# Short convolution, router and experts in one kernel: the inversion's moving operand from one product over three sections, the experts' one-hots written contiguously, past counts added by VectorE, the third block's preparation handed to the first block's loop

## Chip, cores and metric

The kernel runs on one core of one Trainium2 chip. The metric is the device time of one execution in microseconds (us); the median of three runs stands for a kernel. PE is TensorE's matmul side and PEld its weight load, DVE is VectorE, ACT ScalarE, POOL GpSimd and SP the queue that issues most DMAs.

## The reference

```python
# x: (8, 3584, 192) f32, weight: (8, 7); 8 experts, w1: (8, 192, 1024), w2: (8, 1024, 192)
w = softmax(weight)                                   # per head, over 7 taps
y[b, s, h, :] = sum_k w[h, k] * x_padded[b, s + k, h, :]   # causal, 8 heads of 24 channels
t = y.reshape(28672, 192); out = t
do = t @ w_skip > 0                                   # only these tokens go on
e = argmax(t @ w_gate); g = softmax(t @ w_gate)[e]    # one expert of 8 for each
out[do] = t + g * (relu(t @ w1[e]) @ w2[e])           # relu network 192 -> 1024 -> 192
```

## The kernel before

**First phase.** The batches 0 to 7 are taken one after the other. A batch's 3584 tokens lie as 30 columns of 120 partitions. `phase1_step(b)` runs over eight pairs of heads and half-batches: the convolution is a matmul with a banded matrix (`toep`, fp32, L393), which ACT copies into `ys`, and the rows are stored as the preliminary output. Between these steps it advances generators: the router of batch b-1 and the inversion of an earlier batch. A generator gives up its turn at each `yield`; written tables (`RR`, `IR`, `PICK`, `BGS`, `PSEQ`) say how many turns each step gives. Every engine works its own instructions strictly in the order in which this program issued them.

**Router.** `router` turns `ys` by matmuls (`tp`), multiplies by the gate weights (`pl`), turns back (`pb`) and leaves logits `lg`, 120 x 30 x 9. `slots` finds each token's expert and its place in that expert's list. DVE makes `lm`, `df`, `kq`, `km` and then `oh`, an fp16 one-hot of the expert over 30 columns x 8 experts. PE multiplies `oh` by a matrix of ones and by a triangular matrix into the PSUM tile `pr`, and adds the counts of past batches (`hist`) by a third, one-row product. DVE then runs a scan along `pr` (`run`), adds the rest (`rs`), masks with `oh`, and reduces to the slot `sl`. From the slot come a row `rf`, a column `qf` and three small fp16 factors `vv`, `gh`, `gl`, which carry the token number and the gate value.

**Inversion.** `invert(b)` turns "token to slot" into "slot to token" by matmuls. For each chunk of 8 columns (`IC`; four chunks a batch, the last of 6) DVE compares into the stationary operand `oa` and into the moving operand `ob`; `ob` has three sections of 72 columns: the one-hot of `qf` times `vv`, times `gh` and times `gl`. One product per token column adds to the PSUM tile `inv` (L646). After batch 4 (`REL`) the lists of the first two experts are read out of it (`inva`, `sidxa`), so that their first eight blocks can begin early.

**Blocks.** A block is up to 256 tokens of one expert. `gather` fetches its rows, `prep` scales and splits them into fp16 high and low parts (DVE: `yam`, `ysc`, ACT and DVE: `yt`) and turns them by DMA into `m`; `up` is the first expert product (PE `ph`, ACT `hh`, DVE `hl`), `down` the second (PE `po`, DVE `o`, POOL scatter). The first blocks run between the last two batches' routing and inversion: `weave` issues a block's rows and, after each quarter of `up`, a `tail_slot`. During batch 7's convolution `step7(h)` issues `PSEQ[h]` pieces of the preparation of the first three blocks (`prep_piece`); a preparation of 256 tokens has seven pieces. The table sums to 21.

Of the kernel before, what the change touches and what calls it, by code (L numbers as in the profile page):

```python
# [8 lines left out]
F16 = mybir.dt.float16  # L9
# [93 lines left out]
def conv_router_moe(ctx: ExitStack, tc: tile.TileContext, x, weight, w_skip, w_gate, w1, w2, out):  # L103
# [431 lines left out]
    def slots(b, lg):  # L535
        def t3(name):
            return wk1.tile([R, NC, E], F32, tag=name, bufs=1, name=f"{name}{b}")

        def t2(name, dt=F32, bufs=1):
            return wk1.tile([R, NC], dt, tag=name, bufs=bufs, name=f"{name}{b}")  # L540

        def bc(t):
            return t.unsqueeze(2).broadcast_to([R, NC, E])

        lm = t2("lm")
        nc.vector.tensor_reduce(out=lm, in_=lg[:, 0:NC, 0:E], axis=AX.X, op=ALU.max)
        yield
        nc.vector.tensor_tensor(out=lg[:, NC - 1, E:E + 1], in0=lg[:, NC - 1, E:E + 1], in1=live, op=ALU.min)
        df = t3("df")
        nc.vector.tensor_tensor(out=df, in0=lg[:, 0:NC, 0:E], in1=bc(lm), op=ALU.subtract)  # L550
        ex = t3("ex")
        nc.scalar.activation(ex, df, AF.Exp)
        yield
        kq = t3("kq")
        nc.vector.scalar_tensor_tensor(out=kq, in0=df, scalar=0.0,
                                       in1=pri[0:R].unsqueeze(1).broadcast_to([R, NC, E]),
                                       op0=ALU.is_equal, op1=ALU.mult)
        yield
        km = t2("km")
        nc.vector.tensor_reduce(out=km, in_=kq, axis=AX.X, op=ALU.min)  # L560
        yield
        nc.vector.scalar_tensor_tensor(out=km, in0=lg[:, 0:NC, E], scalar=0.0, in1=km,
                                       op0=ALU.is_le, op1=ALU.add)
        yield
        oh = wk1.tile([R, E, NC], F16, tag="oh", name=f"oh{b}")
        nc.vector.tensor_tensor(out=oh.rearrange("p e c -> p c e"), in0=kq, in1=bc(km), op=ALU.is_equal)
        yield HOP
        if in_tail:
            yield HOP
        pr = ps_ms.tile([P, 2, E, NC], F32, tag="ms", name=f"pr{b}")  # L570
        nc.tensor.matmul(pr[:, 0], ones16[0:R, :], oh, start=True, stop=False)
        nc.tensor.matmul(pr[:, 0, :, 0], ones32, hist[0:1, b, :], start=False, stop=True)
        nc.tensor.matmul(pr[0:R, 1], um1[0:R, 0:R], oh, start=True, stop=True)
# [17 lines left out]
        nc.vector.tensor_copy(hist[:, b + 1, :], run[:, :, NC - 1])
        yield
        if b == REL:
            nc.vector.tensor_tensor(out=cnta, in0=hist[:, b + 1, 0:NA], in1=eoff[:, 0:NA], op=ALU.subtract)
            yield
            nc.vector.scalar_tensor_tensor(out=hist[:, b + 1, 0:NA], in0=eoff[:, 0:NA], scalar=float(KH * P),
                                           in1=hist[:, b + 1, 0:NA], op0=ALU.add, op1=ALU.max)
        nc.vector.tensor_tensor(out=rs, in0=rs, in1=oh, op=ALU.mult)
        yield HOP
        sl = t2("sl")  # L600
        nc.vector.tensor_reduce(out=sl, in_=rs.rearrange("p e c -> p c e"), axis=AX.X, op=ALU.add)
# [10 lines left out]
        nc.vector.tensor_tensor(out=eq3(cmp), in0=stab, in1=bstart[:, b].unsqueeze(2).broadcast_to([P, E, QC]),  # L612
                                op=ALU.is_ge)
        rf = t2("rf", F16, 2)
        nc.vector.tensor_copy(rf, ri)
        qf = t2("qf", F16, 2)
        nc.vector.tensor_copy(qf, qi)

        gs, gd = t2("gs"), t2("gd")
        nc.vector.tensor_scalar(out=gs, in0=gt, scalar1=UNITS, scalar2=None, op0=ALU.add)  # L620
        vu, vv = t2("vu"), t2("vv", F16, 2)
        nc.vector.tensor_scalar(out=vu, in0=ai, scalar1=PACK - 1.0, scalar2=1.0, op0=ALU.mult, op1=ALU.add)
        nc.vector.tensor_scalar(out=gs, in0=gs, scalar1=UNITS, scalar2=GBIAS, op0=ALU.subtract, op1=ALU.subtract)
        nc.vector.tensor_tensor(out=vv, in0=vu, in1=vtab[0:R], op=ALU.mult)
        nc.vector.scalar_tensor_tensor(out=gd, in0=gt, scalar=GBIAS, in1=gs, op0=ALU.subtract, op1=ALU.subtract)
        nc.vector.tensor_scalar(out=gd, in0=gd, scalar1=1.0 / PACK, scalar2=UNITS, op0=ALU.mult, op1=ALU.add)
        gh, gl = t2("gh", F16, 2), t2("gl", F16, 2)
        nc.vector.tensor_tensor(out=gh, in0=gs, in1=vu, op=ALU.mult)
        nc.vector.tensor_scalar(out=gd, in0=gd, scalar1=UNITS, scalar2=GREST, op0=ALU.subtract, op1=ALU.min)
        nc.vector.scalar_tensor_tensor(out=gl, in0=gd, scalar=-GREST, in1=vu, op0=ALU.max, op1=ALU.mult)  # L630
        rq[b] = (rf, qf, vv, gh, gl)
# [3 lines left out]
    def invert(b, rf, qf, vv, gh, gl):  # L635


        due = []
# [1 line left out]
        def products(at):  # L640
            if due and due[0][0] <= at:
                _, c0, i, oa, ob = due.pop(0)
                for v in range(min(IL, NC - c0 - IL * i)):
                    w = c0 + IL * i + v
                    at_q = IL * i + v
                    nc.tensor.matmul(inv, oa[:, i, :, v], ob[:, at_q // QL, :, at_q % QL],  # L646
                                     start=(b in (0, REL + 1) and w == 0), stop=(b in (REL, B - 1) and w == NC - 1))

        def each(out, in0, t, c0, op):
# [13 lines left out]
        at = 0  # L663
        for c0 in range(0, NC, IC):
            oa = wk1.tile([R, IC // IL, P, IL], F16, tag="oa", bufs=3, name=f"oa{b}_{c0}")
            ob = wk1.tile([R, IC // QL, 3 * NG, QL], F16, tag="ob", bufs=3, name=f"ob{b}_{c0}")
            each(oa, iota_r, rf, c0, ALU.is_equal)
            yield
            each(ob[:, :, 0:NG, :], iota_q, qf, c0, ALU.is_equal)
            products(at)  # L670
            at += 1
            yield HOP
            for n, part in enumerate((gh, gl)):
                each(ob[:, :, (n + 1) * NG:(n + 2) * NG, :], ob[:, :, 0:NG, :], part, c0, ALU.mult)
            each(ob[:, :, 0:NG, :], ob[:, :, 0:NG, :], vv, c0, ALU.mult)
            products(at)
            due.extend((at + TLAG, c0, i, oa, ob) for i in range(IC // IL))
            at += 1
# [514 lines left out]

    routes.append(whole_route(B - 1))
    in_tail.append(1)
    gathered, prepped = AHEAD - 1, PREP0
    ahead = []
    while preps or begun[0] < PREP0:
        prep_piece()
    bg.extend(save_weights(e, wts[e]) for e in range(NA))  # L1200
    weave(up(blocks[0], weights_of(0)), first=(blocks[0], *FIRSTP[0]))
    for n in range(NBLK):
        k = blocks[n]
        if 0 < n < 5:
# [105 lines left out]
```

## Time and profile before

| | |
|---|---|
| runs | 684.56, 684.56, 689.15 us; median 684.56 us |
| the profiled execution | 686.43 us, span of its instructions 684.7 us |
| mean granted TensorE clock | 0.993 |
| busy | PE 656.2 us (96%), DVE 544.3 (79%), ACT 352.1 (51%), POOL 271.0 (40%) |
| DMA | 133.31 MB, mean 195 GB/s |

The span is the time from the first to the last instruction. A timeline row gives start, length, engine, line, operation, destination and sources, and in brackets the idle time of that engine just before it and what ended that. A group row gives busy time, mean nanoseconds of one instruction and that idle time in total. [...]

### The profile page before, as it was taken

What the parts mean: (1) busy time and instruction counts of PE and PEld (TensorE: products, weight loads), DVE (VectorE), ACT (ScalarE), POOL (GpSimd) and SP (SyncE); (2) the same over time, 40 slices, a digit from 0 to 9 for tenths busy, and PEclk for the clock granted to TensorE, in tenths of its full rate; (3) what the DMA queues carried; (4) which work ended last, traced back from release to release, by engine and by line L of the source; (5) the groups of instructions that cost most, each with busy time, mean ns of one, the idle gap of its engine ahead of it and who ended that gap; (6) DMA issues with size and microseconds to landing.
All of it is one profiled execution on the core that took longest, in us unless ns stands there. A gap on an engine that the chain in (4) does not pass through costs nothing.

```text
span 684.7 us, 17904 instructions
## 1 busy us (share of the span) xinstructions
PE 656.2 (96%) x6586; PEld 563.9 (82%) x6586; DVE 544.3 (79%) x1617; ACT 352.1 (51%) x762; POOL 271.0 (40%) x301
## 2 busy tenths in 40 slices
PE   8999998999697999989999999999999999999995
PEld 7667676766587898979999899999999899999995
DVE  8159999988989989886997897888888876666652
ACT  4776585558742334554464464564554644444421
POOL 4111111124113454644554554644544555554322
PEclk9999999999999999999999999999999999999999
DMA  7999999962941657466359369578567456999970
GB/s 214 322 322 313 300 286 326 326 217 66 246 145 47 161 143 153 89 181 182 82 170 216 89 175 193 105 175 177 126 181 157 132 148 175 272 291 330 326 211 15
DMA packets 169127, 133.31 MB, mean 195 GB/s; under 512 B 74320, under 2 KB 155986, under 8 KB 169028
## 3 DMA queue, kind: packets, MB, share of 16 engines
q1 hardware_dynamic: 157988, 110.26, 60.1%
q0 software_dynamic: 11040, 21.80, 11.8%
q8 instruction: 54, 0.88, 0.5%
q14 instruction: 45, 0.37, 0.2%
HBM read 69.70 MB, written 48.04 MB: 172 GB/s over the span
## 4 chain that ended last, share of the span: by engine, by line
PE 55%; DVE 0%; POOL 0%; POOLq 0%; issue 0%
PE ph L888 28%; PE po L939 27%; POOL out_dram L927 0%; DVE hl L911 0%; POOLq L1251 0%; DVE yt L859 0%; DVE o L925 0%
## 5 line engine op out<-in xcount | busy, mean ns | idle before, releaser
L909 ACT ACTIVATE hh<-ph 128x512 f16<-128x512 f32 x230 | 136.2, 593 | 227.1 <-PE ph L888 226.1
L888 PE MATMUL ph<-m,wt 128*128 128x256 f16 (+2 forms) x2000 | 210.0, 270 | 4.4 <-DVE hl L911 2.8
L888 PEld LDWEIGHTS <-wt 128*128 128x128 f16 (+1 forms) x2000 | 167.5, 98 | 38.7 <-issue 17.9
L939 PE MATMUL po<-wt,hh 128*128 128x192 f16 x1536 | 194.2, 246 | 0.0
L911 DVE SCALAR_TENSOR_TENSOR hl<-ph,hh 128x512 f16<-128x512 f32 x230 | 157.5, 686 | 40.9 <-ACT hh L909 40.5
L939 PE MATMUL po<-wt,hl 128*128 128x192 f16 x768 | 188.9, 246 | 0.0
L939 PEld LDWEIGHTS <-hh 128*128 128x128 f16 x1840 | 166.5, 98 | 1.1
L927 POOL DMA_INDIRECT out_dram<-o,sidx x82 | 85.8, 1046 | 138.7 <-DVE o L925 119.4
L829 POOL DMA_INDIRECT y<-out_dram,sidx x82 | 85.3, 1041 | 26.8 <-issue 10.1
L939 PEld LDWEIGHTS <-hl 128*128 128x128 f16 x920 | 90.0, 98 | 0.0
L393 PE MATMUL pc<-xs,toep 128*120 128x384 f32 (+1 forms) x224 | 77.3, 467 | 0.0
L925 DVE SCALAR_TENSOR_TENSOR o<-po,yf,y 128x192 f32<-128x192 f32 x115 | 47.2, 417 | 37.0 <-PE po L939 30.8
L859 DVE SCALAR_TENSOR_TENSOR yt<-y,ysc,yt 128x64 f16<-128x64 f32 x230 | 62.2, 313 | 14.8 <-ACT yt L853 13.2
L395 ACT COPY ys<-pc 120x768 f32<-120x768 f32 (+1 forms) x56 | 42.6, 761 | 40.7 <-PE pc L393 31.8
L853 ACT ACTIVATE yt<-y,ysc 128x192 f16<-128x192 f32 x115 | 51.4, 447 | 19.4 <-DVE ysc L362 13.8
L393 PEld LDWEIGHTS pc<-xs,toep 128*120 128x120 f32 x224 | 36.5, 183 | 14.1 <-issue 0.4
L854 ACT ACTIVATE yt<-y,ysc 128x128 f16<-128x128 f32 x115 | 44.8, 389 | 0.0
L338 DVE SCALAR_TENSOR_TENSOR wt<-raw,ar,wt 128x512 f16<-128x512 f32 x56 | 42.2, 759 | 1.4 <-ACT wt L327 1.4
L327 ACT ACTIVATE wt<-raw,ar 128x512 f16<-128x512 f32 x56 | 38.9, 724 | 5.3 <-DVE ar L362 5.3
L888 PE MATMUL ph<-m,wd 128*128 128x256 f16 (+3 forms) x440 | 40.6, 258 | 0.0
L939 PE MATMUL po<-wd,hh 128*128 128x192 f16 x304 | 38.4, 246 | 0.0
L888 PEld LDWEIGHTS <-wd 128*128 128x128 f16 (+1 forms) x440 | 32.9, 97 | 6.6 <-issue 3.4
(213 smaller groups left out, 778.8 us busy)
## 6 DMA issues: line engine op xcount, KB each, us to landing
wd<-wscr SPq DMA_DIRECT2D x44, 449.0 KB
wscr<-wt SPq DMA_DIRECT2D x84, 128.0 KB
xs<-in_x_dram SPq DMA_DIRECT2D x7, 1440.0 KB
xs<-in_x_dram SPq DMA_DIRECT2D x7, 1248.0 KB
out_dram<-ys SPq DMA_DIRECT2D x6, 1344.0 KB
out_dram<-ys SPq DMA_DIRECT2D x6, 1092.0 KB
raw<-in_moe_w_dram SPq DMA_DIRECT2D x32, 192.0 KB
raw<-in_moe_w_dram SPq DMA_DIRECT2D x8, 512.0 KB
```

The source lines that it names most:

```text
L393: nc.tensor.matmul(pc[0:R, i, 0:n * G], toep[:, h + i, :], xs[b, half][:, :, (h + i) * G:(h + i + 1) * G], start=True, stop=True)
L395: nc.scalar.copy(ys[b, half][0:R, :, h * G:(h + 2) * G].rearrange("p g (h c) -> p h g c", c=G), pc[0:R, :, 0:n * G].rearrange("p i (g c) - ...
L829: rows_apart(nc.gpsimd.indirect_dma_start(out=k.y[:, u, :], out_offset=None, in_=out[0:k.rows, :], in_offset=bass.IndirectOffsetOnAxis(ap= ...
L853: nc.scalar.activation(yt[:, u, 0:D], k.y[:, u, :], AF.Copy, scale=sc[:, u:u + 1])
L854: nc.scalar.activation(yt[:, u, 3 * P:], k.y[:, u, D - P:D], AF.Copy, scale=sc[:, u:u + 1])
L859: nc.vector.scalar_tensor_tensor(out=yt[:, u, o:o + b_ - a], in0=k.y[:, u, a:b_], scalar=sc[:, u:u + 1], in1=yt[:, u, a:b_], op0=ALU.mult, ...
L888: nc.tensor.matmul(ph[:, f % fs, :], wt[q, o + f * P:o + (f + 1) * P], k.m[q, m, 0:w], start=start, stop=stop, skip_group_check=split)
L909: nc.scalar.activation(hh, ph, AF.Relu)
L911: nc.vector.scalar_tensor_tensor(out=k.hl[:, f0:f0 + fs, 0:w], in0=ph, scalar=0.0, in1=hh, op0=ALU.max, op1=ALU.subtract)
L925: nc.vector.scalar_tensor_tensor(out=o[:, u, :], in0=part, scalar=f2[:, u:u + 1], in1=k.y[:, u, :], op0=ALU.mult, op1=ALU.add)
L927: rows_apart(nc.gpsimd.indirect_dma_start(out=out[0:k.rows, :], out_offset=bass.IndirectOffsetOnAxis(ap=k.si[:, u:u + 1], axis=0), in_=o[: ...
L939: nc.tensor.matmul(part, lhs[:, f, u * P:(u + 1) * P], wt[:, w + f * D:w + (f + 1) * D], start=(n == 0), stop=(n == 3 * NF - 1))
```

## The change

1. `ob`: DVE now compares into a tile `eq` of its own, and one product over the three sections makes `ob`: `eq` is read three times by a broadcast, against a tile `parts` that holds the three factors side by side in pairs of columns. It takes the place of three products, one for each section.
2. `oh` is stored as 30 columns x 8 experts in the order in which DVE computes it, so its write is contiguous. The two matmuls write `pr` as before with experts outermost, now with a pitch of 30 elements between consecutive results. The masking of `rs` reads `oh` with a pitch of 8 elements.
3. The one-row product of `hist` goes; DVE adds the 8 counts to `pr` in front of the scan.
4. At the start of the last batch's routing, the loop that issued what was left of the three preparations goes; what is left is handed to the first block's `weave`.

```diff
-        oh = wk1.tile([R, E, NC], F16, tag="oh", name=f"oh{b}")
-        nc.vector.tensor_tensor(out=oh.rearrange("p e c -> p c e"), in0=kq, in1=bc(km), op=ALU.is_equal)
+        oh = wk1.tile([R, NC, E], F16, tag="oh", name=f"oh{b}")
+        nc.vector.tensor_tensor(out=oh, in0=kq, in1=bc(km), op=ALU.is_equal)
...
-        nc.tensor.matmul(pr[:, 0], ones16[0:R, :], oh, start=True, stop=False)
-        nc.tensor.matmul(pr[:, 0, :, 0], ones32, hist[0:1, b, :], start=False, stop=True)
-        nc.tensor.matmul(pr[0:R, 1], um1[0:R, 0:R], oh, start=True, stop=True)
+        nc.tensor.matmul(pr[:, 0].rearrange("p e c -> p c e"), ones16[0:R, :], oh, start=True, stop=True)
+        nc.tensor.matmul(pr[0:R, 1].rearrange("p e c -> p c e"), um1[0:R, 0:R], oh, start=True, stop=True)
...
+        nc.vector.tensor_tensor(out=pr[:, 0, :, 0], in0=pr[:, 0, :, 0], in1=hist[:, b, :], op=ALU.add)
...
-        nc.vector.tensor_tensor(out=rs, in0=rs, in1=oh, op=ALU.mult)
+        nc.vector.tensor_tensor(out=rs, in0=rs, in1=oh.rearrange("p c e -> p e c"), op=ALU.mult)
...
+        parts = wk1.tile([R, NC // QL, 3, QL], F16, tag="parts", name=f"parts{b}")
...
-        nc.vector.tensor_tensor(out=vv, in0=vu, in1=vtab[0:R], op=ALU.mult)
+        nc.vector.tensor_tensor(out=parts[:, :, 0], in0=by(vu), in1=by(vtab[0:R]), op=ALU.mult)
...
-            each(ob[:, :, 0:NG, :], iota_q, qf, c0, ALU.is_equal)
+            eq = wk1.tile([R, IC // QL, NG, QL], F16, tag="eq", bufs=2, name=f"eq{b}_{c0}")
+            each(eq, iota_q, qf, c0, ALU.is_equal)
...
-            for n, part in enumerate((gh, gl)):
-                each(ob[:, :, (n + 1) * NG:(n + 2) * NG, :], ob[:, :, 0:NG, :], part, c0, ALU.mult)
-            each(ob[:, :, 0:NG, :], ob[:, :, 0:NG, :], vv, c0, ALU.mult)
+            nc.vector.tensor_tensor(out=ob[:, 0:n], op=ALU.mult,
+                                    in0=eq[:, 0:n].unsqueeze(2).broadcast_to([R, n, 3, NG, QL]),
+                                    in1=parts[:, g0:g1].unsqueeze(3).broadcast_to([R, n, 3, NG, QL]))
...
-    gathered, prepped = AHEAD - 1, PREP0
-    ahead = []
-    while preps or begun[0] < PREP0:
-        prep_piece()
+    gathered, prepped = AHEAD - 1, begun[0]
+    ahead = list(preps)
...
-    weave(up(blocks[0], weights_of(0)), first=(blocks[0], *FIRSTP[0]))
+    weave(up(blocks[0], weights_of(0)), ahead, PU, first=(blocks[0], *FIRSTP[0]))
```

The order of instructions before, on DVE, at the first two chunks of batch 0's inversion (a number behind a tile's name only tells buffers apart; the last figures are partitions x elements):

```order
L658 TENSOR_TENSOR oa_0_691<-iota_r,rf_671 120x1024
L658 TENSOR_TENSOR ob_0_692<-iota_q,qf_673 120x4x144
L658 TENSOR_TENSOR ob_0_692<-ob_0_692,gh_685 120x4x144
L658 TENSOR_TENSOR ob_0_692<-ob_0_692,gl_686 120x4x144
L658 TENSOR_TENSOR ob_0_692<-ob_0_692,vv_679 120x4x144
L658 TENSOR_TENSOR oa_8_750<-iota_r,rf_671 120x1024
```

And in the changed kernel, on DVE, from the new addition of the past counts on (rows in between left out are the same small ones as before) and at the same chunks:

```order
L584 TENSOR_TENSOR pr_610<-pr_610,hist 128x8
L586 SCALAR_TENSOR_TENSOR run_637<-smask,pr_610 128x240
...
L662 TENSOR_TENSOR oa_0_689<-iota_r,rf_672 120x1024
L662 TENSOR_TENSOR eq_0_692<-iota_q,qf_674 120x576
L680 TENSOR_TENSOR ob_0_690<-eq_0_692,parts_671 120x1728
L662 TENSOR_TENSOR oa_8_747<-iota_r,rf_672 120x1024
L662 TENSOR_TENSOR eq_8_750<-iota_q,qf_674 120x576
L680 TENSOR_TENSOR ob_8_748<-eq_8_750,parts_671 120x1728
```

Three rows become one at each of 32 chunks, and one row of 8 elements is new in each of 8 batches; no other row of DVE changes its place.

On PE, before, between the turning products of batch 0 (`tp`, from `ys`) and the next convolution product (`pc`):

```order
L571 LDWEIGHTS ones_105
L571 MATMUL pr_610<-oh_590,ones_105 128x240
L572 MATMUL pr_610<-hist,ones_96 128x8
L573 LDWEIGHTS um_238
L573 MATMUL pr_610<-oh_590,um_238 120x240
L393 MATMUL pc_0_4_618<-xs_0_183,toep 120x384 x2
```

And in the changed kernel at the same place:

```order
L574 LDWEIGHTS ones_105
L574 MATMUL pr_610<-oh_590,ones_105 128x30x8
L575 LDWEIGHTS um_238
L575 MATMUL pr_610<-oh_590,um_238 120x30x8
L393 MATMUL pc_0_4_617<-xs_0_183,toep 120x384 x2
```

The one-row product is gone in each of the 8 batches, and the results go out as 30 groups of 8 with a pitch; nothing else moves on PE.

On ACT, at the end of batch 7's convolution, where the third block's preparation (`yt_2373` from `y_2032`) is followed by the last weight pieces and the first block's first `hh`, the kernel before has:

```order
L327 ACTIVATE wt_1108<-raw_1378,ar_1878 128x512
L853 ACTIVATE yt_2373<-y_2032,ysc_2347 128x192
L854 ACTIVATE yt_2373<-y_2032,ysc_2347 128x128
L853 ACTIVATE yt_2373<-y_2032,ysc_2347 128x192
L854 ACTIVATE yt_2373<-y_2032,ysc_2347 128x128
L327 ACTIVATE wt_1108<-raw_1378,ar_1878 128x512 x3
L909 ACTIVATE hh_2412<-ph_0_2414 128x512
L477 COPY ya_0_2431<-tp_0_0_2432 128x480
```

The changed kernel has these eight rows in the same order, with other buffer numbers and line numbers; so have its queues of POOL and SP, row for row.

More of the change, by code (lines that the diff above doesn't have):

```diff
@@ L543, in bc, with by @@
             return t.unsqueeze(2).broadcast_to([R, NC, E])
+        def by(t):
+            return t.rearrange("p (g v) -> p g v", v=QL)
         lm = t2("lm")
@@ L620, in slots, with invert @@
         nc.vector.tensor_scalar(out=gs, in0=gt, scalar1=UNITS, scalar2=None, op0=ALU.add)
-        vu, vv = t2("vu"), t2("vv", F16, 2)
+        vu = t2("vu")
         nc.vector.tensor_scalar(out=vu, in0=ai, scalar1=PACK - 1.0, scalar2=1.0, op0=ALU.mult, op1=ALU.add)
         nc.vector.tensor_scalar(out=gs, in0=gs, scalar1=UNITS, scalar2=GBIAS, op0=ALU.subtract, op1=ALU.subtract)
-        nc.vector.tensor_tensor(out=vv, in0=vu, in1=vtab[0:R], op=ALU.mult)
+        nc.vector.tensor_tensor(out=parts[:, :, 0], in0=by(vu), in1=by(vtab[0:R]), op=ALU.mult)
         nc.vector.scalar_tensor_tensor(out=gd, in0=gt, scalar=GBIAS, in1=gs, op0=ALU.subtract, op1=ALU.subtract)
         nc.vector.tensor_scalar(out=gd, in0=gd, scalar1=1.0 / PACK, scalar2=UNITS, op0=ALU.mult, op1=ALU.add)
-        gh, gl = t2("gh", F16, 2), t2("gl", F16, 2)
-        nc.vector.tensor_tensor(out=gh, in0=gs, in1=vu, op=ALU.mult)
+        nc.vector.tensor_tensor(out=parts[:, :, 1], in0=by(gs), in1=by(vu), op=ALU.mult)
         nc.vector.tensor_scalar(out=gd, in0=gd, scalar1=UNITS, scalar2=GREST, op0=ALU.subtract, op1=ALU.min)
-        nc.vector.scalar_tensor_tensor(out=gl, in0=gd, scalar=-GREST, in1=vu, op0=ALU.max, op1=ALU.mult)
-        rq[b] = (rf, qf, vv, gh, gl)
+        nc.vector.scalar_tensor_tensor(out=parts[:, :, 2], in0=by(gd), scalar=-GREST, in1=by(vu),
+                                       op0=ALU.max, op1=ALU.mult)
+        rq[b] = (rf, qf, parts)
         if b < B - 1:
             nc.vector.scalar_tensor_tensor(out=brow, in0=cmp, scalar=float(S), in1=brow, op0=ALU.mult, op1=ALU.add)
-    def invert(b, rf, qf, vv, gh, gl):
+    def invert(b, rf, qf, parts):
         due = []
@@ L645, in products @@
                     at_q = IL * i + v
-                    nc.tensor.matmul(inv, oa[:, i, :, v], ob[:, at_q // QL, :, at_q % QL],
+                    nc.tensor.matmul(inv.rearrange("p (s q) -> p s q", s=3), oa[:, i, :, v], ob[:, at_q // QL, :, :, at_q % QL],
                                      start=(b in (0, REL + 1) and w == 0), stop=(b in (REL, B - 1) and w == NC - 1))
@@ L665, in invert @@
             oa = wk1.tile([R, IC // IL, P, IL], F16, tag="oa", bufs=3, name=f"oa{b}_{c0}")
-            ob = wk1.tile([R, IC // QL, 3 * NG, QL], F16, tag="ob", bufs=3, name=f"ob{b}_{c0}")
+            ob = wk1.tile([R, IC // QL, 3, NG, QL], F16, tag="ob", bufs=3, name=f"ob{b}_{c0}")
             each(oa, iota_r, rf, c0, ALU.is_equal)
             yield
-            each(ob[:, :, 0:NG, :], iota_q, qf, c0, ALU.is_equal)
+            eq = wk1.tile([R, IC // QL, NG, QL], F16, tag="eq", bufs=2, name=f"eq{b}_{c0}")
+            each(eq, iota_q, qf, c0, ALU.is_equal)
             products(at)
@@ L672, in invert @@
             yield HOP
-            for n, part in enumerate((gh, gl)):
-                each(ob[:, :, (n + 1) * NG:(n + 2) * NG, :], ob[:, :, 0:NG, :], part, c0, ALU.mult)
-            each(ob[:, :, 0:NG, :], ob[:, :, 0:NG, :], vv, c0, ALU.mult)
+            g0, g1 = c0 // QL, min(c0 + IC, NC) // QL
+            n = g1 - g0
+            nc.vector.tensor_tensor(out=ob[:, 0:n], op=ALU.mult,
+                                    in0=eq[:, 0:n].unsqueeze(2).broadcast_to([R, n, 3, NG, QL]),
+                                    in1=parts[:, g0:g1].unsqueeze(3).broadcast_to([R, n, 3, NG, QL]))
             products(at)
```

## The prediction

> **What bounds the kernel now.** I began with the busy times by stage; the columns are the stretch, its length, PE, PEld, DVE, ACT and POOL busy with counts, clock, DMA share and GB/s.
>
> ```profile
> span 684.7 us, 17904 instructions
> 80.00:120.00 40.00, 38.05 (x283) 27.49 (x282) 37.32 (x115) 26.81 (x55) 5.03 (x8) 1.00 0.98 298
> 120.00:160.00 40.00, 37.55 (x280) 27.13 (x279) 35.40 (x108) 22.18 (x49) 8.86 (x15) 1.00 0.76 236
> 160.00:200.00 40.00, 33.71 (x309) 26.38 (x308) 35.63 (x122) 29.79 (x70) 8.89 (x10) 0.96 0.57 160
> 200.00:240.00 40.00, 34.77 (x375) 32.45 (x373) 38.91 (x122) 11.75 (x28) 13.73 (x14) 1.00 0.46 122
> 302.00:677.00 375.00, 374.65 (x4107) 339.72 (x4106) 288.74 (x785) 181.38 (x391) 184.99 (x182) 1.00 0.72 181
> ```
>
> From 302 to 677 us PE is busy for 374.65 of 375 us, and the chain that ended last is there nothing but PE's two expert products, to within a few us of the end:
>
> ```profile
> 302.35 5.64 PE ph L888 x35
> ...
> 673.22 3.97 PE po L939 x48
> ```
>
> The change does not touch that stretch, so it moves as a whole, by what is won before it. From 80 to 240 us PE idles 1.95 + 2.45 + 6.29 + 5.23 = 15.9 us, with DVE busy 147 of 160 us. The time can come only from these holes and from PE's own instructions. The groups and the timeline of PE name the holes:
>
> ```profile
> L571 PE MATMUL pr<-oh,ones 120*128 120x240 f16 x8 | 2.1, 264 | 6.8 <-DVE oh L566 6.8
> L646 PE MATMUL inv<-ob,oa 120*128 120x216 f16 x240 | 31.9, 262 | 4.4 <-DVE ob L658 4.4
> 109.37 0.26 PE L571 MATMUL pr<-oh,ones 120*128 120x240 f16 x1 [1.95 <-DVE oh L566]
> 141.78 0.55 PE L646 MATMUL inv<-ob,oa 120*128 120x216 f16 x4 [1.34 <-DVE ob L658]
> 156.26 0.26 PE L571 MATMUL pr<-oh,ones 120*128 120x240 f16 x1 [1.10 <-DVE oh L566]
> 178.76 1.08 PE L476 MATMUL tp<-ident,ys 120*128 120x120 f32 x8 [2.57 <-ACT ya L477]
> 184.01 0.26 PE L571 MATMUL pr<-oh,ones 120*128 120x240 f16 x1 [2.68 <-DVE oh L566]
> 206.13 0.26 PE L571 MATMUL pr<-oh,ones 120*128 120x240 f16 x1 [1.08 <-DVE oh L566]
> 210.97 1.25 PE L888 MATMUL ph<-m,wt 128*128 128x256 f16 x10 [0.65 <-DVE hl L911]
> 212.74 0.56 PE L646 MATMUL inv<-ob,oa 120*128 120x216 f16 x4 [0.52 <-DVE ob L658]
> 219.81 0.55 PE L646 MATMUL inv<-ob,oa 120*128 120x216 f16 x4 [2.16 <-DVE ob L658]
> 231.64 1.25 PE L888 MATMUL ph<-m,wt 128*128 128x256 f16 x10 [0.41 <-DVE hl L911]
> 238.66 0.56 PE L646 MATMUL inv<-ob,oa 120*128 120x216 f16 x4 [0.42 <-DVE ob L658]
> ```
>
> The 11.2 us behind `oh` and `ob` are exactly where the change works. But DVE is a backlogged queue: a hole closes only by what DVE has saved since it last waited for somebody else. It waits rarely:
>
> ```profile
> 99.79 0.75 DVE L338 SCALAR_TENSOR_TENSOR wt<-raw,ar,wt 128x512 f16<-128x512 f32 x1 [0.52 <-ACT wt L327]
> 150.96 0.38 DVE L687 COPY inva<-inv 128x216 f32<-128x216 f32 x1 [2.55 <-PE inv L646]
> 199.12 0.55 DVE L859 SCALAR_TENSOR_TENSOR yt<-y,ysc,yt 128x64 f16<-128x64 f32 x2 [2.17 <-ACT yt L853]
> ```
>
> Before 99.79 us the holes above don't occur, so what DVE saves for the first batches buys nothing.
>
> **The change part by part.** The DVE rows that price it, by form (mean ns behind the busy time; for L591 minimum, median, maximum):
>
> ```profile
> L658 DVE TENSOR_TENSOR oa<-iota_r,rf 120x1024 f16<-120x1024 f16 x24 | 16.5, 687 | 0.0
> L658 DVE TENSOR_TENSOR ob<-iota_q,qf 120x576 f16<-120x576 f16 x24 | 10.8, 451 | 0.0
> L566 DVE TENSOR_TENSOR oh<-kq,km 120x240 f16<-120x240 f32 x8 | 9.7, 1211 | 0.3
> L555 DVE SCALAR_TENSOR_TENSOR kq<-df,pri 120x240 f32<-120x240 f32 x8 | 3.3, 407 | 0.3
> L601 DVE TENSOR_REDUCE sl<-rs 120x30 f32<-120x240 f32 x8 | 4.7, 590 | 0.1
> L560 DVE TENSOR_REDUCE km<-kq 120x30 f32<-120x240 f32 x8 | 3.2, 403 | 0.3
> L612 DVE TENSOR_TENSOR cmp<-stab,bstart 128x144 f32<-128x144 f32 x8 | 2.4, 301 | 0.0
> L591 DVE COPY hist<-run x8: 162/165/930, 46.5 to 212.9; 128x8 f32<-128x8 f32 x8
> 104.88 0.46 DVE L658 TENSOR_TENSOR ob<-ob,gh 120x576 f16<-120x576 f16 x1
> 106.12 0.40 DVE L546 TENSOR_REDUCE lm<-lg 120x30 f32<-120x240 f32 x1
> 108.11 1.20 DVE L566 TENSOR_TENSOR oh<-kq,km 120x240 f16<-120x240 f32 x1
> 108.94 0.82 DVE L658 TENSOR_TENSOR oa<-iota_r,rf 120x512 f16<-120x512 f16 x2
> ```
>
> *The fused product.* The three products of a chunk hold DVE from 104.88 to 106.12, 1.24 us. In fp16 an element costs (687 - 451) / 448 = 0.53 ns, so 1728 elements take 687 + 704 x 0.53 = 1.06 us, and the next instruction starts some 0.07 us before such a one ends: 0.99 us, **0.25 us saved a chunk**. The nearest rows at the dearer end are the fp32 ones, (407 - 301) / 96 = 1.1 ns an element: 301 + 1584 x 1.1 = 2.04 us, 0.7 us lost a chunk. I take the fp16 rate, since the small factors are read in the same pairs and with the same broadcast over 72 columns in the present rows; the dear end is a rival below.
>
> *`oh` contiguous.* At 240 elements and with the same kind of sources `kq` takes 0.41 against 1.21 us: 0.80 us earlier for PE, which waits for its end. For DVE's queue the saving is less, since its next instruction starts 0.83 us after `oh` (108.11 to 108.94) and would start some 0.32 after it: 0.51 us.
>
> *What is added on DVE.* The 8-element addition is like L591, and the scan waits for its end: 0.2 us. `rs` now reads `oh` with a pitch; `sl` reads with a pitch of 30 elements and takes 590 where `km` takes 403, so 0.18 us (from 0 to the 0.80 that `oh` paid for writing with a pitch). The three writes into `parts` go in pairs with gaps: between 0 and (1211 - 407) / 240 = 3.4 ns for 30 elements, 0.1 us each; I take 0.1 for the three. Together 0.48 us a batch.
>
> *On PE* the one-row product goes:
>
> ```profile
> 44.72 0.38 PE L572 MATMUL pr<-hist,ones 1*128 1x8 f32 x2
> 45.03 0.31 PE L573 MATMUL pr<-oh,um 120*120 120x240 f16 x1
> ```
>
> That is 0.31 us a batch. Against it stand two products of 240 columns that write PSUM with a pitch of 30 fp32 elements, which no row of before does at length. Ends: nothing, and 0.80 us each, as for `oh`. The nearest row in pitch and element size is `sl`, so 0.19 us each: PE comes out 0.07 us a batch worse, practically even.
>
> [...]
>
> *The third block's preparation* costs nothing and brings nothing: a preparation has seven pieces, the table issues 21, and so all three are issued before the removed loop; what is handed on is an exhausted list. In the order of ACT, POOL and SP nothing changes. The 2.57 us hole at 178.76, behind ACT's work on that block, stays but for what reaches ACT earlier.
>
> **The sum**, as the lead over before, at each hole the smaller of PE's and DVE's. At 109: three batches of -0.07 on PE give -0.2; DVE adds two chunks and `oh`, 0.5 + 0.8, so 1.1 (PE alone could have used 1.95). At 141.8: DVE's own lead is -0.2 + 0.5 + 0.51 = 0.8, then six chunks 1.5, one more `oh` 0.51, two batches of additions -0.96: 1.85, less than PE's 2.3. Until 150.96 PE leads and DVE waits. At 156: + 0.8, 2.65. To 178.8: DVE's 1.85 + 0.51 - 0.48 + 0.5 = 2.4, carried by ACT. At 184: one chunk and `oh`, 3.4. At 206: DVE had waited for ACT at 199, so again one chunk and `oh`, 4.5. From there to 219.8 chunks and additions cancel, 4.4. At 231.6 and 238.7 the four last chunks are worth more than the two holes, + 0.8: **5.2 us**. What comes behind has no hole that the change reaches.
>
> The profiled execution took 686.43 us, its span and 1.7 around it, and lies 1.9 us above the median of 684.56; the lead is the same on both, so the forecast is 684.56 - 5.2 = **679.4 us** (681.2 on the profiled execution's scale). With the small terms at their kinder or harsher ends it lies between 675 and 683.
>
> **Rivals.**
> - *All named holes close and the pitched writes are free.* 6.8 + 4.4 us and 8 x 0.31: 13.7 us, 670.9. For it speaks that DVE saves 8 x (1.0 + 0.5 - 0.5) = 8 us in all; against it that the holes at 109, 141 and 219 are larger than what DVE saves ahead of them. 12 in 100.
> - *The pitched writes cost PE as much as `oh` cost DVE,* 0.80 us each: 1.3 us a batch worse, 10.4 in all. PE then arrives later, and the holes absorb most of it; walking the same places gives -2.6 at 109, -3.9 at 141, -2.4 at 184, -1.8 at the end: 686.4, no measurable change. [...] 14 in 100.
> - *The fused product falls to the fp32 rate:* slower. It then holds DVE 1.97 us instead of 1.24 for a chunk of 8, and decides from about 1.40 us an instruction, where the gain is used up. The late chunks of DVE's stretches carry it: 5 us late at 141.8, of which 2.55 us of DVE's wait hide nearly two, 6 at 184, 8.5 at 219.8, 10 at the end: 694.5. For it: one operand repeats whole rows in the middle of its pattern, which no row shows. Against it: the other operand's pattern is today's, at 0.53 ns an element. [...] 8 in 100.
> - *The change doesn't do what it says* holds for the preparation, for certain, and is in the sum at zero.
>
> **How the numbers follow.** The forecast has 63 in 100, the rivals 12, 14 and 8, and 3 are left for what I don't see. About 1% (6.8 us) is what a measurement of this kernel can tell from no change, so the bound lies at 677.7, inside the forecast's own range: I put 30 of its 63 below it. Faster: 30 + 12 = 42. Within 1%: 33 + 14 + 1 = 48. Slower: 8 + 2 = 10. The range runs from the first rival to the second, 671 to 686.5; the third is left out, with the edges of the others.
>
> **What would show it.** `oh` near 0.41 us and the fused product near 1.06; `rs`'s masking between 0.41 and 0.6; PE's holes behind `oh` down from 6.8 to about 3 us and behind `ob` from 4.4 to about 2; the hole in front of `tp` near 178 still over 2 us; PE's chain of expert products beginning near 297 instead of 302.35. On PE the second `pr` product would start 0.31 us nearer to the first if the first's pitched write is free, 0.1 us nearer at my price, 0.5 us further away with the second rival. I would be wrong if DVE's saving were eaten by a wait that I count as covered: the new addition stands in front of the scan, and behind both stand the slots of the batch, the next `oa` and `ob`, and PE's `inv`.

## The result, and the profile after

The changed kernel takes 676.2 us (median of five, 674.65 to 677.63) where the kernel before takes 684.56 (median of five, 683.08 to 689.15): 8.4 us less by the medians; the ratio is 0.9864 with a 95% interval of 0.9837 to 0.989, which makes 9.3 us. The forecast of 679.4 had the direction and a range that holds the time; the size was 3.2 us short. The profiled execution took 674.65 us, so the two traces differ by 11.8 us: the one of before lies 1.9 us above its median, that of after 1.5 below.

The stretches of after that answer to those of before (length, PE, PEld, DVE, ACT and POOL busy with counts, clock, DMA share, GB/s), and the two ends of the unbroken stretch in the chain that ended last:

```profile
80.00:120.00 40.00, 39.43 (x292) 28.54 (x290) 36.35 (x105) 28.59 (x60) 6.44 (x8) 1.00 0.96 294
120.00:160.00 40.00, 39.69 (x308) 28.75 (x308) 35.03 (x117) 25.31 (x55) 10.98 (x18) 1.00 0.75 233
160.00:200.00 40.00, 36.26 (x340) 29.61 (x339) 37.22 (x108) 26.37 (x63) 7.96 (x8) 0.96 0.67 188
200.00:240.00 40.00, 36.63 (x397) 34.47 (x395) 38.05 (x128) 14.01 (x32) 17.32 (x18) 1.00 0.44 113
302.00:665.00 363.00, 363.00 (x4003) 330.08 (x4001) 281.16 (x764) 177.73 (x383) 178.90 (x176) 1.00 0.71 183
```

```profile
292.33 3.97 PE ph L895 x35
...
661.54 3.97 PE po L946 x48
```

From 302 us on nothing has changed but the place: PE is full, and the stretch as a whole lies earlier. It begins at 292.33 instead of 302.35, a lead of 10.0 us. The last 1.7 us between the traces come from its first row, 3.97 us now and 5.64 before; the granted clock was 1.00 there now and 0.50 before, so this is a matter of the clock, not of the change (last section). From 80 to 240 us PE now idles 0.57 + 0.31 + 3.74 + 3.37 = 8.0 us instead of 15.9. The groups of PE's products that wait for `oh` and `ob`, and PE's timeline where holes stood or still stand:

```profile
L574 PE MATMUL pr<-oh,ones 120*128 120x240 f16 x8 | 2.9, 364 | 1.1 <-DVE oh L569 0.9
L650 PE MATMUL inv<-ob,oa 120*128 120x216 f16 x240 | 32.1, 263 | 2.6 <-DVE ob L680 2.6
107.41 0.36 PE L574 MATMUL pr<-oh,ones 120*128 120x240 f16 x1 [0.57 <-DVE oh L569]
151.60 0.36 PE L574 MATMUL pr<-oh,ones 120*128 120x240 f16 x1 [0.31 <-DVE oh L569]
173.16 1.86 PE L476 MATMUL tp<-ident,ys 120*128 120x120 f32 x8 [2.51 <-ACT ya L477]
177.35 0.36 PE L574 MATMUL pr<-oh,ones 120*128 120x240 f16 x1
178.57 1.04 PE L476 MATMUL tp<-ident,yc 120*128 120x120 f32 x8 [0.65 <-ACT yc L459]
197.49 0.36 PE L574 MATMUL pr<-oh,ones 120*128 120x240 f16 x1
210.90 0.55 PE L650 MATMUL inv<-ob,oa 120*128 120x216 f16 x4 [2.11 <-DVE ob L680]
```

Behind `oh` 0.9 us are left of 6.8, behind `ob` 2.6 of 4.4. Three holes of before have no bracket any more: the `inv` at 141.78, and the `pr` products that stood at 184.01 and 206.13 and now stand at 177.35 and 197.49. The two that the forecast left open are still there in full: 2.51 us in front of `tp` and 2.11 us in front of the late `inv`; one of 0.65 us in front of the `yc` products is new. The lead over before, read at the same instruction in both timelines:

| first `pr` product, or as named | before | after | lead | forecast |
|---|---|---|---|---|
| at 109 | 109.37 | 107.41 | 1.96 | 1.1 |
| at 156 | 156.26 | 151.60 | 4.66 | 2.65 |
| `tp` at 179 | 178.76 | 173.16 | 5.60 | 2.4 |
| at 184 | 184.01 | 177.35 | 6.66 | 3.4 |
| at 206 | 206.13 | 197.49 | 8.64 | 4.5 |
| late `inv` | 219.81 | 210.90 | 8.91 | 4.4 |
| chain of expert products | 302.35 | 292.33 | 10.02 | 5.2 |

These are one execution against one. In the trace of experiment 4, whose instructions are those of before, the product at 109 starts at 109.38, that at 156 at 157.74 and that at 206 at 205.27: a lead in the middle of the table is good to about 1.5 us, that at 109 is far better. The lead is above the forecast from the first hole on and the excess grows, so what was missed doesn't lie in one wait alone.

At the first hole the excess can be taken apart. The turning products in front of it, before and then after, with the last row of DVE that waited for another engine ahead of the hole (at 99.79 before):

```profile
106.43 0.98 PE L476 MATMUL tp<-ident,ys 120*128 120x120 f32 x8
```

```profile
105.85 0.99 PE L476 MATMUL tp<-ident,ys 120*128 120x120 f32 x8
99.21 0.75 DVE L338 SCALAR_TENSOR_TENSOR wt<-raw,ar,wt 128x512 f16<-128x512 f32 x1 [0.52 <-ACT wt L327]
```

PE is 0.58 us earlier, and DVE's queue starts earlier by the same 0.58; the hole is 1.38 us smaller. The forecast had -0.2 for the first and 1.3 for the second. So here nearly all that was missed comes from PE.

What DVE pays now (mean ns behind the busy time; for L601 minimum, median, maximum), and where it now waits:

```profile
L680 DVE TENSOR_TENSOR ob<-eq,parts 120x1728 f16<-120x1728 f16 x24 | 26.0, 1085 | 0.4
L569 DVE TENSOR_TENSOR oh<-kq,km 120x240 f16<-120x240 f32 x8 | 3.3, 408 | 0.3
L584 DVE TENSOR_TENSOR pr<-pr,hist 128x8 f32<-128x8 f32 x8 | 1.3, 166 | 0.3 <-PE pr L575 0.3
L601 DVE TENSOR_TENSOR rs<-rs,oh x8: 575/603/615, 46.7 to 204.2; 120x240 f32<-120x240 f32 x8
124.09 0.40 DVE L549 TENSOR_REDUCE lm<-lg 120x30 f32<-120x240 f32 x1 [0.39 <-ACT lg L510]
```

The fused product takes 1085 ns (priced 1.06 us; the mean holds one row of 1.77, and 22 of the 24 took 1.03 to 1.06), `oh` 408 (0.41), the addition 166 (0.2 with its wait), the masking 603 (priced 0.18 more than the 408 of before, got 0.195). Row by row the prices were right. At 124.09 DVE now waits for the logits `lg`, where before its timeline shows no wait between 99.79 and 150.96: its backlog is gone by then, and PE and ACT ahead of it set its pace.

What `oh` frees in DVE's queue was priced too low. The second group of rows behind `oh` before (`oh` itself at 108.11), and the same place after:

```profile
109.68 0.38 DVE L658 TENSOR_TENSOR ob<-iota_q,qf 120x432 f16<-120x432 f16 x1
```

```profile
106.94 0.41 DVE L569 TENSOR_TENSOR oh<-kq,km 120x240 f16<-120x240 f32 x1
107.27 0.62 DVE L662 TENSOR_TENSOR oa<-iota_r,rf 120x512 f16<-120x512 f16 x2
107.81 0.38 DVE L662 TENSOR_TENSOR eq<-iota_q,qf 120x432 f16<-120x432 f16 x1
```

`oh` at 106.94 lasts 0.41 us and the next row starts 0.33 us after it: rows overlap here, so the queue is counted from start to start. From `oh` to there it was 1.57 us and is 0.87: 0.70 us, where the forecast had 0.51. The rows right behind the pitched write were slower too: the two `oa` took 0.82 us and take 0.62. In five of the eight batches the row behind `oh` is 0.2 us shorter now; in that of 155 us, where a copy follows, it is not. What is added in DVE's queue, from start to start, is 0.2 us for the addition and 0.21 for the masking, nothing for `parts`: 0.41 instead of 0.48.

The other term that was not right stands on PE. The slot of the `pr` group in batch 0, from its first product to the next convolution product, before and after:

```profile
44.53 0.26 PE L571 MATMUL pr<-oh,ones 120*128 120x240 f16 x1
45.18 0.49 PE L393 MATMUL pc<-xs,toep 128*120 128x384 f32 x1
```

```profile
44.72 0.37 PE L574 MATMUL pr<-oh,ones 120*128 120x240 f16 x1
44.88 0.41 PE L575 MATMUL pr<-oh,um 120*120 120x240 f16 x1
45.08 1.50 PE L393 MATMUL pc<-xs,toep 128*120 128x384 f32 x4
```

It was 0.65 us and is 0.36, with 0.04 more that the following products lose (four of them last 1.50 us where they lasted 1.46): 0.25 us less a batch, where the forecast had 0.07 more. The slot was 0.65 or 0.66 us in seven of the eight batches of before.

### The profile page after: what moved, and what is told of

It reads as the page before. It is cut to its first block, busy times and chain, and to the rows that moved or that the text cites. A ratio compares the mean times of both kernels' runs of the same rounds, so it can differ in the third digit from the quotient of the medians.

```text
span 672.8 us, 17815 instructions
## 1 busy us (share of the span) xinstructions
PE 652.8 (97%) x6570; PEld 562.1 (84%) x6570; DVE 533.1 (79%) x1561; ACT 352.0 (52%) x762; POOL 272.1 (40%) x301
## 4 chain that ended last, share of the span: by engine, by line
PE 55%; DVE 0%; POOL 0%; POOLq 0%; issue 0%
PE ph L895 28%; PE po L946 27%; POOL out_dram L934 0%; DVE hl L918 0%; POOLq L1256 0%; DVE yt L866 0%; DVE o L932 0%
```

## The experiments

**The theories.** P: what PE saves in its own instructions lasts to the end, because DVE's and ACT's work starts from PE's results and moves with it. D: PE's saving only enlarges the next hole behind DVE, and only what DVE saves counts. The forecast's walk, "at each hole the smaller of PE's and DVE's", is close to D. First each edit was done alone on the kernel before; the four ran on one chip, against 685.37 us for the kernel before. Three dots mark lines of an edit that are left out.

**1. The fused product alone** (with the fourth edit, which moves no instruction):

```diff
...
-            for n, part in enumerate((gh, gl)):
-                each(ob[:, :, (n + 1) * NG:(n + 2) * NG, :], ob[:, :, 0:NG, :], part, c0, ALU.mult)
-            each(ob[:, :, 0:NG, :], ob[:, :, 0:NG, :], vv, c0, ALU.mult)
+            nc.vector.tensor_tensor(out=ob[:, 0:n], op=ALU.mult,
+                                    in0=eq[:, 0:n].unsqueeze(2).broadcast_to([R, n, 3, NG, QL]),
+                                    in1=parts[:, g0:g1].unsqueeze(3).broadcast_to([R, n, 3, NG, QL]))
...
```

> The kernel before with the fused product alone (the one-hots and the counts as before). Theory D (the gain is what DVE saves, given back at PE's holes): 0.25 us a chunk, 0.5 us of lead at the hole near 109 us, 1.8 at 141, 2.6 at 184, 2.9 at 206, some 4 at the end: 3 to 4.5 us faster than before. Theory P (the gain beyond the forecast is PE's own, because the pitched PSUM writes are free): the same here, since PE's instructions are as before. Rival (the fused product only moves the wait): 0 to 1 us faster, with PE's holes behind ob as large as before.

Measured: 681.29 us, ratio 0.9936 [0.9905, 0.9966], 4.4 us less. The groups:

```profile
L574 PE MATMUL pr<-oh,ones 120*128 120x240 f16 x8 | 2.2, 276 | 5.7 <-DVE oh L569 5.7
L650 PE MATMUL inv<-ob,oa 120*128 120x216 f16 x240 | 32.1, 263 | 2.8 <-DVE ob L680 2.8
```

The 0.25 us a chunk shows mostly in the holes behind `ob`, 2.8 us of 4.4; those behind `oh` keep 5.7 of 6.8. In this trace the lead is 0.56 us at the hole at 109 and 1.24 at 141 (0.5 and 1.8 were expected), but only 1.35 at the chain of expert products: this execution took 684.92 us, 3.6 above the median, and its clock was 0.50 from 182 to 189 us, twice as long as in the trace of before. The size is read from the medians alone. The third rival, a fall to the fp32 rate, is out: 1.05 us a product here too.

**2. `oh` contiguous alone,** with the one-row product kept:

```diff
...
-        nc.tensor.matmul(pr[:, 0], ones16[0:R, :], oh, start=True, stop=False)
+        nc.tensor.matmul(pr[:, 0].rearrange("p e c -> p c e"), ones16[0:R, :], oh, start=True, stop=False)
         nc.tensor.matmul(pr[:, 0, :, 0], ones32, hist[0:1, b, :], start=False, stop=True)
...
```

> The kernel before with the contiguous one-hots alone (pitched PSUM writes, the one-row product kept). Theory D: the holes behind oh shrink by 0.8 us each, in DVE's queue 0.5 less 0.2 for the pitched read: 2 to 3.5 us faster. Theory P: as D, and the two pr products take PE no longer than before. If the pitched writes cost 0.19 us each, PE's lead falls by 3 us over the batches wherever PE is the later one, and the gain is under 2 us.

Measured: 680.89 us, ratio 0.9946 [0.9925, 0.9966], 3.7 us less. The slot of PE in batch 0:

```profile
44.44 0.37 PE L571 MATMUL pr<-oh,ones 120*128 120x240 f16 x1
44.73 0.38 PE L572 MATMUL pr<-hist,ones 1*128 1x8 f32 x2
45.05 0.41 PE L573 MATMUL pr<-oh,um 120*120 120x240 f16 x1
45.26 1.17 PE L393 MATMUL pc<-xs,toep 128*120 128x384 f32 x3
```

The slot is 0.82 us instead of 0.65; with the 0.04 after it the two pitched writes cost 0.2 us together, where the forecast had 0.38. So the pitched writes are neither free nor 0.19 us each. The holes behind `oh` fall to 2.5 us.

**3. The past counts added by DVE alone:**

```diff
-        nc.tensor.matmul(pr[:, 0], ones16[0:R, :], oh, start=True, stop=False)
-        nc.tensor.matmul(pr[:, 0, :, 0], ones32, hist[0:1, b, :], start=False, stop=True)
+        nc.tensor.matmul(pr[:, 0], ones16[0:R, :], oh, start=True, stop=True)
...
+        nc.vector.tensor_tensor(out=pr[:, 0, :, 0], in0=pr[:, 0, :, 0], in1=hist[:, b, :], op=ALU.add)
```

> The kernel before with the past counts added by DVE alone. PE saves 0.31 us a batch, DVE takes 0.2 us a batch more. Theory D: the holes are DVE's, so PE's saving only makes the next hole larger, and DVE's addition makes it later: from 0.5 us faster to 1 us slower. Theory P taken by itself (PE's saving counts wherever it is made): 2 to 2.5 us faster.

Measured: 681.57 us, ratio 0.9958 [0.9939, 0.9976], 2.9 us less. This is the run that decides between the theories: it takes work from PE and gives DVE some, so by D there was next to nothing to win. PE's slot and the groups with the holes:

```profile
44.55 0.26 PE L571 MATMUL pr<-oh,ones 120*128 120x240 f16 x1
44.65 0.26 PE L572 MATMUL pr<-oh,um 120*120 120x240 f16 x1
44.75 1.45 PE L393 MATMUL pc<-xs,toep 128*120 128x384 f32 x4
L571 PE MATMUL pr<-oh,ones 120*128 120x240 f16 x8 | 2.1, 264 | 7.4 <-DVE oh L566 7.4
L646 PE MATMUL inv<-ob,oa 120*128 120x216 f16 x240 | 31.9, 262 | 4.8 <-DVE ob L658 4.8
```

The slot falls from 0.65 to 0.20 us: the one-row product had cost 0.45 us, not the 0.31 that I read off between two starts. Eight of them are 3.6 us, and the holes grew by only 0.6 + 0.4 = 1.0 us. D falls. The lead read in this trace is 1.16 us at the hole at 109, 2.16 at 184 and 2.63 at the chain of expert products. At 109 the hole is 1.94 us where it was 1.95: `oh` came earlier by as much as PE did. Up to the chain this trace has one stretch of half clock, as that of before has.

**4. The preparation's hand-over alone:**

```diff
...
-    while preps or begun[0] < PREP0:
-        prep_piece()
+    ahead = list(preps)
...
```

> The kernel before with the fourth edit alone. Both theories: the same instructions in the same order, so 0 us; what it differs by is the scatter of these measurements (within 1.5 us). Rival (the spread preparation works as it is named): the hole near 178 us, 2.57 us, shrinks, 1 to 3 us faster.

Measured: 685.08 us, ratio 1.0012 [0.9991, 1.0033]. Nothing, and the hole is where it was:

```profile
179.45 1.86 PE L476 MATMUL tp<-ident,ys 120*128 120x120 f32 x8 [2.57 <-ACT ya L477]
```

The three that do something sum to 4.4 + 3.7 + 2.9 = 11.0 us; the whole change, by its ratio, is worth 9.3. With an uncertainty of 1.3 to 2.1 us on each, they add up as far as these runs can tell.

**5. The size of a pitched write.** In the changed kernel the product of ones is repeated six times with contiguous and seven times with pitched results, the last of which leaves what the scan reads:

```diff
-        nc.tensor.matmul(pr[:, 0].rearrange("p e c -> p c e"), ones16[0:R, :], oh, start=True, stop=True)
+        for _ in range(6):
+            nc.tensor.matmul(pr[:, 0].rearrange("p e c -> p (e c)"), ones16[0:R, :], oh, start=True, stop=True)
+        for _ in range(7):
+            nc.tensor.matmul(pr[:, 0].rearrange("p e c -> p c e"), ones16[0:R, :], oh, start=True, stop=True)
```

> The changed kernel with the disputed write by itself: in each batch the first pr product is issued 13 times, 6 times with contiguous results and then 7 times with the pitch of 30 elements (the last one counts). From start to start the contiguous ones should take 0.10 us (240 columns, as the two pr products do where the one-row product is left out and the results are contiguous). If pitched writes are free, 0.10 as well; by the changed kernel's spacing (0.16 and 0.20) 0.16 to 0.20; by my price in the prediction 0.29; by the second rival 0.9.

```profile
44.45 0.78 PE L575 MATMUL pr<-oh,ones 120*128 120x240 f16 x6
45.06 1.58 PE L577 MATMUL pr<-oh,ones 120*128 120x240 f16 x7
46.44 0.41 PE L578 MATMUL pr<-oh,um 120*120 120x240 f16 x1
```

Only the trace of this run is read, not its time. From start to start, six contiguous ones take 0.61 us, 0.102 each, and seven pitched ones 1.38, 0.197 each: half the rate, 0.095 us dearer. My price of 0.19 was twice that, the second rival's 0.80 eight times.

**6. A pitched read in place of the pitched write.** The two products take their columns from `oh` with a pitch of 16 bytes and write contiguously:

```diff
-        nc.tensor.matmul(pr[:, 0].rearrange("p e c -> p c e"), ones16[0:R, :], oh, start=True, stop=True)
+        nc.tensor.matmul(pr[:, 0], ones16[0:R, :], oh.rearrange("p c e -> p e c"), start=True, stop=True)
...
```

> The changed kernel with the pitch on the other side of the two pr products: they read the one-hots with a pitch of 8 fp16 elements and write PSUM contiguously. The pitched write cost 0.10 us a product in the run before (0.197 against 0.102 from start to start). If the pitched read is free on PE, the two products are 0.10 us apart and the kernel is 0.8 to 1.6 us faster than the changed one; if it costs what the write does, the same within 0.5 us; if it costs what DVE pays for pitched reads (0.19 us and more), slower by 1.5 us or more.

```profile
44.83 0.59 PE L574 MATMUL pr<-oh,ones 120*128 120x240 f16 x1
45.23 0.61 PE L575 MATMUL pr<-oh,um 120*120 120x240 f16 x1
45.66 1.47 PE L393 MATMUL pc<-xs,toep 128*120 128x384 f32 x4
```

0.40 and 0.43 us a product: four times the contiguous one and twice the pitched write. Of the two ways to have `oh` contiguous for DVE, the change took the cheaper; the late `inv` starts at 213.15 us here and at 210.62 in the changed kernel on the same chip. The time, 703.36 us, ratio 0.9869 [0.9803, 0.9936], cannot tell it from the change itself, for the following reason.

**Other chips.** This run, that of section 5 and all that follow ran on three other chips, on which the kernel before takes 710 us. Up to some 215 us the changed kernel's trace there agrees with that of the first chip to 0.3 us; from then on PE idles at times inside the expert products for nothing that the profile shows:

```profile
219.10 0.24 PE L946 MATMUL po<-wt,hh 128*128 128x192 f16 x1 [0.48 <-issue]
```

The changed kernel once more on such a chip: 703.53 us against 710.49, ratio 0.9925 [0.989, 0.996].

> The changed kernel once more, on the chip of the next two runs, as their base: 1.0 to 1.6% faster than before on any chip, since the gain was made before 215 us of the trace.

The gain is smaller there, 5.3 us or 0.75% by that ratio, under the 1.0 to 1.6% that were expected. Times between the variants differ by less than this spread, so what decides is where instructions start up to 213 us.

**7. In the whole change, the one-row product back on PE:**

```diff
-        nc.tensor.matmul(pr[:, 0].rearrange("p e c -> p c e"), ones16[0:R, :], oh, start=True, stop=True)
+        nc.tensor.matmul(pr[:, 0].rearrange("p e c -> p c e"), ones16[0:R, :], oh, start=True, stop=False)
+        nc.tensor.matmul(pr[:, 0, :, 0], ones32, hist[0:1, b, :], start=False, stop=True)
...
-        nc.vector.tensor_tensor(out=pr[:, 0, :, 0], in0=pr[:, 0, :, 0], in1=hist[:, b, :], op=ALU.add)
```

> The changed kernel with the one-row product put back in place of DVE's addition. The third experiment made the one-row product look dearer than its 0.31 us: without it the two pr products and what follows began 0.45 us earlier a batch. Theory P (the gain beyond the forecast is PE's own time): PE is the later engine nearly everywhere in the changed kernel, so 8 x 0.45 = 3.6 us come back, less what the remaining holes absorb: 2 to 3.6 us slower than the changed kernel, 678.5 to 680. Theory D (the gain beyond the forecast is DVE's, whose additions are cheaper than I counted): DVE gets 0.2 us a batch back, so within 1 us of the changed kernel, 675.5 to 677.

> The changed kernel with the one-row product in place of DVE's addition, once more beside the changed kernel on one chip. Theory P: 2 to 3.6 us slower than the changed kernel, with the second-phase chain some 3 us later in the trace. Theory D: within 1 us of it.

> The changed kernel with the one-row product of the past counts back on PE in place of DVE's addition. By the slots of PE the product costs 0.45 us in each of eight batches. Theory P (PE's saving lasts to the end): the time is 2.7 to 3.6 us longer than the changed kernel's 676.2, a ratio to the kernel before of 0.990 to 0.992. Theory D (the next hole takes it): the changed kernel's own ratio, 0.986, within 0.002. On a chip where PE shows idle time of the kind 'issue' in the expert products, only the starts up to 213 us decide: the late inv product stands near 213.4 instead of 210.9 by P, near 211 by D.

Measured on three chips: 701.52 us, ratio 0.9855 [0.9814, 0.9897]; 702.95, 0.9894 [0.9845, 0.9942]; 702.37, 0.992 [0.9886, 0.9953]. By what was expected of each, the first is on D's side, the second too (702.95 us beside the 703.53 of the changed kernel on the same chip), the third on P's: by the times this stays open. By where the instructions start it doesn't. The late `inv` in the changed kernel on the second chip, then in this variant on the same chip:

```profile
210.62 0.55 PE L650 MATMUL inv<-ob,oa 120*128 120x216 f16 x4 [2.10 <-DVE ob L680]
```

```profile
213.36 0.55 PE L650 MATMUL inv<-ob,oa 120*128 120x216 f16 x4 [2.03 <-DVE ob L680]
```

The one-row product puts PE 1.40 us behind at the hole at 107, 2.19 at 151 and 2.74 here, with the same hole in front and one stretch of half clock ahead in either trace. In the other two runs of this variant the same instruction starts at 214.32 and 213.02. So six or so of the eight 0.45 us arrive at this place, as P has it; what the idle time on those chips makes of them afterwards isn't seen in the medians.

**8. Removing the hole in front of `tp`.** As the change's fourth edit moves nothing, the table was changed so that it does: none of the third block's pieces is issued in the last step of batch 7's convolution. A second variant also gives the other work between the steps, weight pieces among it, two turns a step instead of one in the second half of batch 7, so that less of it is left behind:

```diff
-PSEQ = (0, 0, 4, 3, 4, 3, 4, 3)
+PSEQ = (0, 0, 4, 3, 4, 3, 4, 0)
...
-BGS = (...) + ("11111111",) * 3
+BGS = (...) + ("11111111", "11111111", "11112222")
```

> The changed kernel with a table that really leaves three pieces of the third block's preparation to the first block's loop (the last entry of the table 0 instead of 3). The hole in front of tp near 173 us, 2.51 us, stands behind ACT's four copies for that block (1.6 us) and their wait for DVE (1.08 us). Theory (the hole is ACT's queue): it shrinks by 1 to 2.5 us, the half-clock stretch behind it may go too, and the kernel is 1 to 3 us faster than the changed one, 673 to 675. Rival (DVE's backlog, the four weight pieces in front of lm, takes the hole's place behind oh): within 1 us, 675.5 to 677.

> As the run before, and the weight pieces left over at the end of the first phase (three on ACT, four on DVE in one piece) are issued two at a time in the second half of batch 7. Theory (ACT's queue): the hole near 173 us goes to below 0.5 us and the half clock with it: 2 to 4.5 us faster than the changed kernel, 671.5 to 674. Rival (DVE's backlog): the pieces now delay ob for batch 6's inversion and the hole reappears in front of inv: within 1.5 us of the changed kernel.

Measured: 704.0 us, ratio 0.9886 [0.9847, 0.9926], and 703.6, ratio 0.990 [0.9859, 0.994]; beside 0.9925 and 0.9864 of the changed kernel itself, no gain. In the first variant the hole in front of `tp` is gone, and this stands in its place:

```profile
177.57 0.36 PE L574 MATMUL pr<-oh,ones 120*128 120x240 f16 x1 [3.17 <-DVE oh L569]
180.05 1.86 PE L476 MATMUL tp<-ident,yc 120*128 120x120 f32 x8 [1.91 <-ACT yc L459]
```

The `pr` product that stood at 177.35 with no hole now waits 3.17 us for `oh`, and ACT is late for `yc` right after. In the second variant the same two products wait 1.64 and 1.91 us. So the 2.51 us were not ACT's piece of preparation alone: in both variants PE then waits for other work of DVE and ACT, and moving a piece moves the wait. No variant beat the changed kernel.

## Why the prediction was right, and which terms were mis-sized

- **Where the time lies** was right: the stretch from 302 us moved as a whole, and the holes behind `oh` and `ob` paid. They went to 0.9 and 2.6 us where I had said about 3 and about 2.
- **DVE's rows** were priced right to within 0.03 us each: 1085 ns against 1.06 us, 408 ns against 0.41, 0.195 against 0.18, 166 ns against 0.2. The three writes into `parts` take 182 to 191 ns each, little over the 174 of `qf`, which is as large and written without gaps; the 0.1 us set aside for them wasn't needed.
- **`oh` in DVE's queue, "some 0.32 after it: 0.51 us",** is a term that was too small: it looked at the first row behind `oh` only. In the queue the contiguous `oh` saves 0.70 us, and what is added costs 0.41 instead of 0.48, so DVE saves some 0.26 us a batch more than forecast in most batches.
- **"PE comes out 0.07 us a batch worse, practically even"** is the term that was furthest off, on both sides. The one-row product was taken at 0.31 us, the distance from its start to the start of the next; experiment 3 shows that taking it away gives back 0.45, since the products around it lose time too. The pitched writes were taken at 0.19 us each from a DVE row; experiments 2 and 5 show 0.1. So PE saves 0.25 us a batch, 0.32 more than forecast, 2.6 us in eight batches. Not all of that arrives: in experiment 3 it was 2.63 of 3.6 us.
- **How far the two terms go.** Put into the forecast's own walk, the measured sizes (PE 0.25 better, `oh` 0.70, additions 0.41) give 2.05 us at 109, 4.1 at 156 and about 7 at the end instead of 5.2, an estimate. That is 1.8 of the 3.2 us by which the forecast was short on the medians, and of the 4.8 in the traces. The rest stays open. Some of it in the traces is scatter: `hist`, 8 elements, took 0.93 us at 134.26 before and 0.16 at the same place after, for no reason that the rows show.
- **The walk along the holes** may have been too strict besides: behind the first hole it gave DVE its own lead alone. Experiment 3 shows that what PE gains mostly reaches DVE too, and the new wait at 124.09 shows DVE caught up with its suppliers. What this is worth wasn't measured apart.
- **The marker on PE** was misleading: I had said that a second `pr` product 0.31 us nearer to the first would show a free pitched write. It is 0.34 us nearer (0.50 to 0.16), and the write isn't free; the marker had the wrong 0.31 in it.
- **The preparation** was right: no effect, and the hole in front of `tp` stayed at 2.51 us.
- **The rivals.** Closing all the holes (670.9) was too much: 2.11 us stayed in front of the late `inv`, where the forecast had put a limit. At 141 and 109, where it had put the other two, the hole closed in full and to 0.57 us. The dear pitched write (686.4) and the fp32 rate (694.5) are refuted by experiments 5 and 1. The fused form keeps the fp16 rate: (1085 - 451) / 1152 = 0.55 ns an element from the 576 elements of one section to three, against 0.53 between the old forms.
- **The chain of expert products** begins at 292.33, not near 297; on medians the lead is 8.4 us.

## What to carry to other kernels

Price a small instruction that is to be removed by the slot of its whole group, from the first of it to the next stranger, and not by the distance between two starts: its neighbours lost time with it here (0.45 us against 0.31). On DVE likewise: read what a slow write costs at the second row behind it, because the first was slower too (0.62 us against 0.42). When a saving on one engine seems bound to vanish in the next wait for another, ask where that other engine's own work starts; if it starts from the first one's results, the saving can travel with it (2.63 of 3.6 us in experiment 3). And before moving work away from in front of a hole, look whether the engine that causes it has other work of the same length behind: in the first variant of experiment 8, 3.17 and 1.91 us of waiting stood where 2.51 had gone.

## What the runs showed of the hardware that was not expected

**The clock falls behind some holes, not behind the same ones in each execution.** Both kernels have a hole of 1.75 us in front of the 35 products that begin the last stretch. The slices right behind it, before and then after (the last three columns are clock, DMA share and GB/s):

```profile
304.00:305.00 1.00, 1.00 (x7) 0.68 (x5) 0.57 (x1) 0.40 (x1) 0.69 (x2) 0.50 0.80 124
```

```profile
294.00:295.00 1.00, 1.00 (x12) 0.90 (x10) 0.59 (x1) 0.78 (x2) 0.69 (x2) 1.00 0.99 136
```

In one execution the clock is 0.50 and 7 products pass in a microsecond, in the other it is 1.00 and 12 pass: 5.64 against 3.97 us for the 35. In the execution of experiment 4, whose instructions are those of before, this place has the full clock, in that of experiment 1 the half one. Such a stretch lasts some 3.5 us and costs up to 1.7; in the traces of experiments 1 and 2 one lasts about 7 us (from 182) and about 10 (from 178). Going by this cost, which holes have one makes up part of the 3 us by which executions of one kernel scatter: an estimate. In the trace of before such a stretch stands behind the holes of 2.68 us (at 184) and 1.75 (at 302), in that of after behind the one of 2.51 (at 173); behind those of 2.57 (at 179) and 2.16 (at 220) before and of 2.11 (at 211) after the clock stays at 1.00. So the length of a hole alone doesn't tell; what does was not shown.

**Pitches on PE,** for 240 columns, from start to start: contiguous 0.10 us and results pitched by 120 bytes 0.20 (experiment 5), moving operand pitched by 16 bytes 0.40 to 0.43 (experiment 6).

**Behind the pitched write on DVE the next row was slower.** Behind `oh` written with a pitch of 60 bytes, the first `oa` row took 0.62 to 0.64 us in four batches; behind the contiguous `oh` it takes 0.42.

**Chips differ.** On the chip of experiments 1 to 4 the kernel before took 685 us, on three others 710, with the idle time named above in the expert products; why is open. Those three also ran last, so chip and time can't be told apart here.
